# A two-layer decode kernel: the first feed-forward takes the up half by column blocks and w_out by matching row blocks, in turns

## The chip, the cores and the metric

The kernel runs on one core of a Trainium2 chip. Its engines are PE (TensorE, with its weight loads shown as PEld), DVE (VectorE), ACT (ScalarE), POOL (GpSimd) and SP (SyncE, which here issues nearly all DMAs). The metric is the device time of one execution in microseconds (us).

## The reference, cut to what matters

One token for each of two sequences passes twice through attention over a cache of 4096 keys and values (16 heads of 256) and a gated feed-forward of 448 to 1792 to 448. The same weights and caches serve both layers.

```python
def _A_ref(x, k_cache, v_cache, wq, wo):
    q = (x @ wq).reshape(B, Sq, H, Dh).transpose(0, 2, 1, 3)
    scores = jnp.einsum("bhqd,bhkd->bhqk", q, k_cache) * (Dh ** -0.5)
    o = jnp.einsum("bhqk,bhkd->bhqd", _softmax(scores), v_cache)
    return o.transpose(0, 2, 1, 3).reshape(B, Sq, H * Dh) @ wo
def _B_ref(x, W_gate, W_up, W_down):
    gate, up = x @ W_gate, x @ W_up
    return ((gate * (gate > 0)) * up) @ W_down
...
x = x + _A_ref(_layernorm(x), A_k_cache, A_v_cache, A_wq, A_wo)
x = x + _B_ref(_layernorm(x), B_W_gate, B_W_up, B_W_down)
# and the same two lines once more; B = 2, Sq = 1, D = 448, H = 16, Sk = 4096, Dh = 256, F = 1792, fp32
```

## The kernel before, in words

Everything that comes from memory lies in one large tile, `arena`, cut into 27 units (`Arena`, L49). A load takes a unit, or several, and the unit is free again when the last reader of the load is in the program. All loads stand in one list, `pending` (L267 and L268), in the order in which they are used. `release` (L206) frees a unit and calls `pump` (L138), which issues the next loads of the list on SP's queue as long as a unit is free. SP's DMA then waits on the chip for the readers of the unit that it overwrites. So each load is issued when an earlier piece has been read, and the loads start in the order of the list.

The program is: attention of layer 1 (32 pairs of head and sequence), the first feed-forward `ffn(False, oT)`, attention of layer 2, and the last feed-forward `ffn(True)`. Layer 2 starts with the pairs with which layer 1 ended, and the arena keeps part of their keys and values (`KEPT`, `LEFT`). Therefore few units circulate in the first feed-forward: the first four pieces of its weights go to four units, and each later piece waits for a release.

A piece of the feed-forward is 128 rows of 1792 floats (896 KB). There are seven pieces of `w_in` and four of `w_out`, the last of them half as large (`ffn_loads`, L247). Pieces 0 to 2 of `w_in` are the gate weights of three blocks of 128 input rows, piece 3 holds the last 64 input rows of gate and up together, and pieces 4 to 6 are the up weights. The hidden vector of 1792 is held as four groups of 448 columns on four groups of 32 partitions, so that four matmuls of 32 columns fill the array side by side (`proj`, L919). Between the gate pieces `arrive` (L939) adds the last head's output to the input.

The first feed-forward then works as follows. The gate sum `pg` goes through a ReLU on ACT into `hid` (L1023). The up sum `pu` is made of pieces 3, 4, 5 and 6 (L1024), with the sums of columns of the next query's weights (`add_up`, L978), the scale of the layer norm (`factors`, L1000) and a part of the output sum `y` put between them by `between` (L960). When all of `pu` is there, DVE multiplies 448 columns at once (L1025). PE turns `hid` by three transposes and two matmuls (L1035, L1037), DVE and ACT copy it back (L1041, L1046).

`w_out` lies by column blocks of the output (128, 128, 128 and 64 wide), each with all 1792 hidden rows as 14 chunks. `block` (L1051) adds 14 matmuls for a column block in the bank `po[1]`. After each block ACT copies it out with its sum (L1125), PE turns it into columns of `x` (L1137), DVE adds it (L1140), and `ask` (L1107) adds one step of the first query of layer 2, `q`. After the last block come the mean's part of the query (L1141), two last steps (L1114), a copy of the query (L496), and then the first scores of layer 2 on DVE (L592, and POOL at L499). Those scores read kept keys, and their readers are what the next loads wait for.

`acc` is the bank in which the heads' outputs are summed, on partitions 0 to 95 in three groups of 32; `y`, the running sum of the residual, is on two partitions from 96 on.

Of the kernel before, what the change touches and what calls it, by code (L numbers as in the profile page):

```python
# [81 lines left out]
def two_layers(  # L82
# [7 lines left out]
    w_out: bass.AP,  # L90
    out: bass.AP,
# [25 lines left out]
    def source(key, n):  # L117
        kind, name, c = key
        if kind in "kv":
            h, b = name  # L120
            at = (h * B + b + (kind == "v")) % (H * B)
            if name in spared and n == PAIR:
                return vk[at, :, VALUES * DH : PAIR * UNIT - KEYS * DH]
            size = F if key in left_at else n * UNIT
            c += NC * (kind == "k" and n < PAIR)
            return vk[at, :, c * UNIT : c * UNIT + size]
        if kind == "g":
            return w_pair[name - 1]
# [138 lines left out]
    pending += of_first + [(key, 1) for key in ffn_loads]  # L267
# [636 lines left out]
    def ffn(last, oT=None):  # L904
# [14 lines left out]
        def proj(p, parts):  # L919

            p = p[:, :D]
            for n, (part, c, done) in enumerate(parts):
# [11 lines left out]
                if not last and n == part and n + 2 <= FULL:  # L934
                    arrive(n + 2)
# [24 lines left out]
        def between(part, n):  # L960


            if last:
                if part in (4, 5):
                    busy(4 if part == 4 else 6)
            elif part == FULL and n == 0:
                factors()
                for i in range(2):
                    nc.tensor.matmul(
                        y, oT[:, i, :], wo[:, i * D : (i + 1) * D], start=False, stop=False  # L970
                    )
            elif part == 4:
                add_up(0)
                add_up(1)
            elif part == 5:
                add_up(2)
# [30 lines left out]

        if not last:
            arrive(0)
            arrive(1)  # L1010
        pg = proj(banks[0], [(0, 0, True), (1, 1, True), (2, 2, True), (3, 3, False)])
# [7 lines left out]
        else:  # L1019
            total = squares()  # L1020
            cols = room_q
        hid = row[:, :D]
        nc.scalar.activation(hid, pg, AF.Relu)  # L1023
        pu = proj(banks[1], [(3, 4, True), (4, 0, True), (5, 1, True), (6, 2, True)])  # L1024
        nc.vector.tensor_mul(hid, pu, hid)  # L1025
        if last:
            unit = ident[SUMS : SUMS + B, SUMS : SUMS + B]
            nc.tensor.matmul(y_left, unit, left, start=True, stop=False)
        else:
            add_up(FULL)  # L1030

        ph = banks[0][:, : FULL * P].rearrange("p (m r) -> p m r", m=FULL)
        ph_tail = small(P)
        for m in range(FULL):
            nc.tensor.transpose(ph[:, m, :], hid[:, m * P : (m + 1) * P], ident)  # L1035
        for half in (0, TAIL):
            nc.tensor.matmul(  # L1037
                ph_tail[half : half + TAIL], hid[:, FULL * P :], ident, start=True, stop=True
            )
        hT = row[:, : FULL * P].rearrange("p (m r) -> p m r", m=FULL)  # L1040
        nc.vector.tensor_copy(hT, ph)  # L1041

        tails = row[:, FULL * P : FULL * P + 64].rearrange("p (m r) -> p m r", m=2)
        for k, half in enumerate((slice(0, TAIL), slice(TAIL, P))):
            pairs = ph_tail[half].rearrange("p (m k r) -> p k m r", m=2, k=2)
            nc.scalar.activation(tails[half], pairs[:, k], AF.Copy)  # L1046
# [17 lines left out]
        if last:  # L1064


            square = little("square", B, bufs=1)
            nc.vector.tensor_mul(square, rstd, rstd)
            close = little("close", CLOSE, B, bufs=1)
            for i, st in enumerate(stat[-CLOSE:]):  # L1070
                nc.vector.tensor_mul(
                    close[:, i, :], square, st.rearrange("p (b r) -> p b r", b=B)[:, :, 0]
                )
            y_end = spare[1][SUMS : SUMS + B, :TAIL]
            nc.tensor.matmul(y_end, unit, y_end_row, start=True, stop=False)
            pds = [po[0][:, :D], spare[0][:, :D]] * 2

            def to_y(at, stop):
                nc.tensor.matmul(y[:, at], scaled, down[:, at], start=False, stop=stop)

            for c in range(FULL):
                at = block(pds[c], c, range(14))
                release("out", "", c)
                nc.scalar.activation(down[:, at], pds[c][:, at], AF.Copy)
                if c > 0:
                    to_y(before, False)
                before = at
            at = block(pds[FULL], FULL, range(14 - CLOSE))
            nc.scalar.activation(down[:, at], pds[FULL][:, at], AF.Copy)
            to_y(before, True)  # L1090
            nc.vector.tensor_copy(left, y_left)
            nc.sync.dma_start(found[:, : FULL * P], left)
            w = get("out", "", FULL)
            for i in range(CLOSE):
                k = 14 - CLOSE + i
                w_k = w[:, k * TAIL : (k + 1) * TAIL]
                nc.tensor.matmul(y_end, close[:, i, :], w_k, start=False, stop=False)
            nc.tensor.matmul(y_end, scaled, down[:, at], start=False, stop=True)
            nc.vector.tensor_copy(y_end_row, y_end)
            nc.scalar.dma_start(found[:, FULL * P :], y_end_row)  # L1100
            return

        q = po[0][:, :DH]

        def ask(c):  # L1107
            x_c = xT[:, c, b : b + 1].to_broadcast([P, P])
            if c < FULL:
                w_c = w_q[:, c * DH : (c + 1) * DH]  # L1110
                nc.tensor.matmul(q, x_c, w_c, start=(c == 0), stop=False)
            else:
                at = (c - FULL) * P
                nc.tensor.matmul(  # L1114
                    q[:, at : at + P], x_c, w_q[:, FULL * DH : FULL * DH + P],
                    start=False, stop=(c == FULL + 1),
                )

        pd = po[1][:, :D]
        sums = little("sums4", FULL + 1, bufs=1)  # L1120
        total = little("sums", 1)
        for c in range(FULL + 1):
            at = block(pd, c, range(14))
            release("out", "", c)
            nc.scalar.activation(down[:, at], pd[:, at], AF.Copy, accum_out=sums[:, c : c + 1])  # L1125
            if c > 0:
                ask(c - 1)
            else:
                add_up(FULL + 1)
            if c == FULL:  # L1130
                turn_cols = row[:, :DH]
                nc.vector.tensor_scalar_mul(turn_cols, cols, nscaled[:, b : b + 1])
                nc.vector.reduce_sum(total, sums, axis=AX.X)
            pt = small(B)
            found_in = [(spans[0][0], c)] if c < FULL else [(p, i.start) for p, i in spans[1:]]
            for p, _ in found_in:
                nc.tensor.matmul(pt[p], down[:, at], scaled, start=True, stop=True)  # L1137
            for p, i in found_in:
                x_c = xr[p, i]
                nc.vector.tensor_add(x_c, x_c, pt[p, :, None].to_broadcast(x_c.shape))  # L1140
        nc.tensor.matmul(q, total.to_broadcast([P, P]), turn_cols, start=False, stop=False)  # L1141
        for c in range(FULL, DC):
            ask(c)

        def center():
            minus = small(B)
            nc.tensor.matmul(minus, total.to_broadcast([P, P]), nscaled, start=True, stop=True)
            add_rows(P, scaled, down)
            less = little("less", B)
            nc.scalar.activation(less, minus, AF.Copy)  # L1150
            squared = little("total", B)
            unread = little("sq4", FULL + 1, bufs=1)
            for i in range(B):
                for p, c in spans:
                    x_c = xr[p, c, i]
                    nc.scalar.activation(x_c, x_c, AF.Identity, bias=less[p, i : i + 1])
                nc.scalar.activation(
                    unread, xT[:, : FULL + 1, i], AF.Square, accum_out=squared[:, i : i + 1]
                )
            nc.scalar.activation(xs[:, :, 32], xs[:, :, 31], AF.Copy)  # L1160
            return squared

        def rest_of_y():
            for c in range(2):
                nc.tensor.matmul(
                    y, oT[:, c, :], means[:, c : c + 1].to_broadcast([P, D]),
                    start=False, stop=False,
                )

        return q, center, rest_of_y  # L1170
# [76 lines left out]
```

## Time and profile before

| what | value |
|---|---|
| time, median of 3 runs | 1314.57 us (1314.09 to 1314.92) |
| the profiled execution's own time | 1314.77 us |
| span of its trace, first to last instruction | 1312.9 us |
| moved from memory | 559.55 MB, 426 GB/s over the span |
| busy share of the span | DVE 82%, PE 39%, POOL 22%, ACT 15% |
| DMA queue of SP | its packets fill 99.4% of 16 engines' span |
| feed-forward of layer 1 in the trace | gate from 665 us, first scores of layer 2 at 689.57 us |

The span is 1.9 us shorter than the time of the same execution. A busy share is an average over the whole span; what matters for the change is read from the 25 us between 665 and 690 us and from what follows. GB/s in a stretch counts the packets that start in it.

### The profile page before, as it was taken

The numbers are of one execution on the slowest core, as the hardware profiler recorded it, in microseconds if no ns is written. First come the engines' busy times: TensorE is split into PE (matmuls) and PEld (weight loads), VectorE is DVE, ScalarE is ACT, GpSimd is POOL, SyncE is SP. The second block draws the span as 40 slices with busy tenths as digits, with TensorE's granted clock in tenths as the row PEclk, the third lists the DMA queues.
The fourth block names the chain that finished last, engine by engine and source line by source line (L and its number), as shares of the span: only waits on it lengthen the run. The fifth ranks groups of instructions, "written<-read, shape, count | busy, mean of one in ns | idle before, by whom it ended". The sixth has DMA issues, their size and how long they took to land.

```text
span 1312.9 us, 8389 instructions
## 1 busy us (share of the span) xinstructions
PE 509.6 (39%) x3056; PEld 156.0 (12%) x3056; DVE 1078.9 (82%) x623; ACT 197.9 (15%) x803; POOL 289.3 (22%) x169
## 2 busy tenths in 40 slices
PE   3142243332433224324485544332343322433348
PEld 2010010010101001101141111000111000110013
DVE  4989989799897998788829798798999889886891
ACT  2100000010000000122417532000000000012231
POOL 0330412302023050021002235140345004100230
PEclk9676777657776567767697766666676667766569
DMA  9999999999999999999999999999999999999998
GB/s 407 437 434 428 438 432 429 437 426 430 444 423 436 441 434 416 446 420 428 421 375 412 433 430 438 437 432 428 429 438 430 437 430 429 440 429 425 434 421 331
DMA packets 20356, 560.09 MB, mean 427 GB/s; under 512 B 2264, under 2 KB 2396, under 8 KB 7260
## 3 DMA queue, kind: packets, MB, share of 16 engines
q1 hardware_dynamic: 20308, 559.56, 99.4%
q8 instruction: 24, 0.39, 0.1%
q14 instruction: 16, 0.13, 0.0%
q10 hardware_dynamic: 8, 0.00, 0.0%
HBM read 559.55 MB, written 0.00 MB: 426 GB/s over the span
## 4 chain that ended last, share of the span: by engine, by line
DMA 52%; DVE 33%; POOL 7%; PE 5%; issue 2%; ACT 1%; SPq 0%; POOLq 0%; DVEq 0%; ACTq 0%
DMA arena<-in_vk_dram 48%; DVE tiny L541 16%; DVE arena L527 10%; POOL tiny L643 5%; DVE arena L576 3%; DMA arena<-in_w_in_dram 3%; POOL tiny L615 2%; PE po L676 1%; DVE arena L592 1%; DMA arena<-in_w_out_dram 1%; PE small L709 1%; DVE tiny L589 1%; ACT arena L582 1%; DVE row L698 1%; DVE tiny L603 0%
## 5 line engine op out<-in xcount | busy, mean ns | idle before, releaser
L527 DVE TENSOR_TENSOR arena<-arena 128x8192 f32<-128x8192 f32 (+2 forms) x53 | 450.4, 8500 | 100.9 <-DMA arena<-in_vk_dram 99.6
L541 DVE TENSOR_REDUCE tiny<-arena 128x32 f32<-128x8192 f32 (+1 forms) x54 | 436.6, 8085 | 0.0
L676 PE MATMUL po<-arena,down 128*4 128x512 f32 x2044 | 316.6, 739 | 180.0 <-ACT down L631 110.6
L615 POOL PARTITION_ALL_REDUCE tiny<-tiny x63 | 96.0, 1524 | 711.9 <-DVE tiny L609 711.2
L709 PE MATMUL small<-tiny,row 128*128 128x2 f32 x124 | 30.6, 351 | 566.7 <-DVE row L698 566.7
L643 POOL PARTITION_ALL_REDUCE tiny<-tiny x63 | 165.3, 2623 | 60.3 <-ACT down L631 60.3
L627 ACT ACTIVATE tiny<-tiny 128x1 f32<-128x1 f32 x63 | 18.5, 294 | 723.7 <-POOL tiny L615 723.7
L676 PEld LDWEIGHTS po<-arena,down 128*4 128x4 f32 x2044 | 66.9, 98 | 401.0 <-issue 229.4
L709 PEld LDWEIGHTS small<-tiny,row 128*128 128x128 f32 x124 | 27.9, 314 | 595.9 <-DVE row L698 595.9
L582 ACT ACTIVATE arena<-arena 128x256 f32<-128x256 f32 x142 | 57.1, 404 | 44.5 <-DVE arena L576 43.6
L456 PE MATMUL po<-arena,xs 128*33 128x512 f32 (+1 forms) x130 | 62.8, 640 | 0.0
L468 POOL PARTITION_BROADCAST arena<-arena x32 | 21.8, 749 | 176.3 <-ACT arena L464 165.5
L732 PE MATMUL acc<-arena,tiny 128*2 128x448 f32 x124 | 50.0, 903 | 23.3 <-DVE tiny L722 23.3
L533 ACT ACTIVATE arena<-arena 128x256 f32<-128x256 f32 x112 | 44.8, 402 | 79.9 <-DVE arena L527 79.9
L576 DVE TENSOR_TENSOR arena<-arena 128x2048 f32<-128x2048 f32 (+2 forms) x21 | 40.2, 1913 | 2.9 <-PE acc L732 2.9
L464 ACT ACTIVATE arena<-po 33x512 f32<-33x512 f32 x13 | 7.7, 590 | 174.6 <-PE po L456 174.6
L722 DVE TENSOR_TENSOR tiny<-small,tiny 128x4 f32<-128x4 f32 x31 | 5.0, 162 | 28.0 <-PE small L709 28.0
L631 ACT ACTIVATE down<-tiny 128x32 f32<-128x32 f32 x64 | 26.6, 415 | 2.2
L582 ACT ACTIVATION_READ_ACCUMULATOR arena<-arena 128x1 f32 x142 | 26.5, 187 | 0.0
L698 DVE SCALAR_TENSOR_TENSOR row<-po,tiny,row 128x256 f32<-128x256 f32 x32 | 15.3, 479 | 13.2 <-ACT row L694 13.1
L456 PEld LDWEIGHTS po<-arena,xs 128*33 128x33 f32 x130 | 16.0, 133 | 59.9 <-issue 57.1
L609 DVE TENSOR_REDUCE tiny<-tiny 128x1 f32<-128x32 f32 x64 | 11.9, 186 | 11.8 <-ACT arena L582 8.5
(207 smaller groups left out, 356.4 us busy)
## 6 DMA issues: line engine op xcount, KB each, us to landing
arena<-in_vk_dram SPq DMA_DIRECT2D x17, 4096.0 KB, 38.8
arena<-in_vk_dram SPq DMA_DIRECT2D x16, 2048.0 KB, 31.1
arena<-in_w_pair_dram SPq DMA_DIRECT2D x11, 1792.0 KB, 30.8
arena<-in_w_in_dram SPq DMA_DIRECT2D x12, 896.0 KB, 25.6
arena<-in_vk_dram SPq DMA_DIRECT2D x10, 1024.0 KB, 9.3
arena<-in_vk_dram SPq DMA_DIRECT2D x1, 6528.0 KB
arena<-in_w_head_dram SPq DMA_DIRECT2D x7, 896.0 KB, 31.5
arena<-in_w_out_dram SPq DMA_DIRECT2D x5, 896.0 KB, 8.5
```

Source lines behind the costliest of these rows:

```text
L456: nc.tensor.matmul(q[:, cols], xs[:, c, :], w_c, start=(i == 0), stop=(i == len(parts) - 1))
L527: nc.vector.tensor_mul(part, part, q_of[u][:, None, :].to_broadcast([P, n, DH]))
L533: nc.scalar.activation(kt[:, t, :], kt[:, t, :], AF.Copy, accum_out=s_of[u][:, t : t + 1])
L541: nc.vector.reduce_sum(found, part, axis=AX.X)
L576: nc.vector.tensor_mul(part[:, :whole, :], kt[:, :whole, :], q_of[u][:, None, :].to_broadcast([P, whole, DH]),)
L582: nc.scalar.activation(part[:, t, :], part[:, t, :], AF.Copy, accum_out=found[:, t : t + 1])
L615: nc.gpsimd.partition_all_reduce(mx_of[u], mx, P, RED.max)
L643: nc.gpsimd.partition_all_reduce(total[:, b : b + 1], rs, P, RED.add)
L676: nc.tensor.matmul(po_of[u][32 * t : 32 * t + 4, (i - 2 * t) * DH : (j - 2 * t) * DH], p_of[u][:, at : at + 4], values[:, i * DH : j * DH] ...
L698: nc.vector.scalar_tensor_tensor(row[:, :DH], po_of.pop(u)[:, DH:], fold[:, 1:2], row[:, :DH], op0=ALU.mult, op1=ALU.add,)
L709: nc.tensor.matmul(pT_of[u][:, c, :], row[:, c * P : (c + 1) * P], pick[:, b : b + B], start=True, stop=True,)
L732: nc.tensor.matmul(acc[at : at + B], oT_of[h][:, c, :], wo[:, c * D : (c + 1) * D], start=(n < 3), stop=(n >= n_u - (5 if settle else 3)),)
```

## The change

The loads of the first feed-forward get another order and two new arrays: `w_up` (the up half by blocks of 128 hidden columns of each of the four groups, and one piece with the 64 last rows of gate beside the last 64 columns of up) and `w_down` (`w_out` by rows: four chunks of 128 hidden rows with all 448 output columns in a piece, the last piece two chunks). The pieces have the sizes of before and their number is 11 as before; the last feed-forward still reads `w_in` and `w_out`.

In the middle, for each block m of hidden columns: the up sum of these columns (`up`), a multiplication by DVE of 128 columns, one transpose, a copy by ACT, and four matmuls 448 wide with piece m of `w_down`. These add in partitions 0 to 95 of `acc`, whose sum stays open from the first turn to the last. After the last turn all four column blocks of that sum are copied, turned and added to `x` one after the other, and the query is asked.

```diff
+        if kind == "up":
+            return w_up[:, c * F : (c + 1) * F]
+        if kind == "dn":
+            return w_down[:, 4 * D * c : min(4 * D * (c + 1), 14 * D)]
...
-    pending += of_first + [(key, 1) for key in ffn_loads]
+    at_turn = [*ffn_loads[:FULL], ("up", "", FULL)]
+    at_turn += [(kind, "", m) for m in range(FULL) for kind in ("up", "dn")] + [("dn", "", FULL)]
+    pending += of_first + [(key, 1) for key in at_turn]
...
+        def tail_of(out, w, width):
+            for j in range(4):
+                i = j % 2 * width
+                nc.tensor.matmul(
+                    out[32 * j : 32 * j + 32, :], xs[:, FULL + j // 2, :32], w[:, i : i + width],
+                    start=False, stop=True,
+                )
+
+        def middle(hid, ph, hT, tails, turn_tail):
+            q = po[0][:, :DH]
+            pu = po[1][:, :D]
+            pd = acc[:SUMS]
+            def up(m, w):
...
+                for c in range(FULL):
+                    for j in range(4):
+                        i = (4 * c + j) * width
+                        nc.tensor.matmul(
+                            pu[32 * j : 32 * j + 32, at], xs[:, c, :32], w[:, i : i + width],
+                            start=(c == 0), stop=False,
+                        )
+                tail_of(pu[:, at], w[:, 4 * FULL * width :], width)
+                nc.vector.tensor_mul(hid[:, at], pu[:, at], hid[:, at])
+                return at
+            up(FULL, get("up", "", FULL)[:, F // 2 :])
+            release("up", "", FULL)
+            factors()
...
+            for m in range(FULL + 1):
+                if m < FULL:
+                    at = up(m, get("up", "", m))
+                    release("up", "", m)
+                    add_up((0, 1, 4)[m])
+                    if m == 0:
+                        turn_tail()
+                    nc.tensor.transpose(ph[:, m, :], hid[:, at], ident)
+                    nc.scalar.activation(hT[:, m, :], ph[:, m, :], AF.Copy)
+                    stat = [hT[:, m, 32 * j : 32 * j + 32] for j in range(4)]
+                else:
+                    nc.vector.tensor_scalar_mul(turn_cols, cols, nscaled[:, b : b + 1])
+                    stat = [tails[:, i, :] for i in range(2)]
...
+                w = get("dn", "", m)
+                for j, st in enumerate(stat):
+                    k = 4 * m + j
+                    g = 32 * (k % 3)
+                    nc.tensor.matmul(
+                        pd[g : g + 32], st, w[:, j * D : (j + 1) * D], start=(k < 3), stop=(k > 10)
+                    )
+                release("dn", "", m)
...
+            for c in range(FULL + 1):
+                at = slice(c * P, c * P + (P if c < FULL else TAIL))
+                nc.scalar.activation(
+                    down[:SUMS, at], pd[:, at], AF.Copy, accum_out=sums[:SUMS, c : c + 1]
+                )
...
+                for p, _ in found_in:
+                    nc.tensor.matmul(
+                        pt[p], down[:SUMS, at], scaled[:SUMS], start=True, stop=True
+                    )
...
+                if c > 0:
+                    ask(c - 1)
...
-        for c in range(FULL + 1):
-            at = block(pd, c, range(14))
             release("out", "", c)
-            nc.scalar.activation(down[:, at], pd[:, at], AF.Copy, accum_out=sums[:, c : c + 1])
...
```

In SP's queue this is the stretch from the first weights of the feed-forward to the first loads of layer 2. Before it reads:

```order
L162 DMA arena<-in_w_in_dram 128x1792 x7
L162 DMA arena<-in_w_out_dram 128x1792 x3
L162 DMA arena<-in_w_out_dram 128x896
L162 DMA arena<-in_w_head_dram 128x1792
L162 DMA arena<-in_vk_dram 128x1792 x2
L162 DMA arena<-in_w_head_dram 128x1792
```

And now:

```order
L168 DMA arena<-in_w_in_dram 128x1792 x3
L168 DMA arena<-in_w_up_dram 128x1792 x2
L168 DMA arena<-in_w_down_dram 128x1792
L168 DMA arena<-in_w_up_dram 128x1792
L168 DMA arena<-in_w_down_dram 128x1792
L168 DMA arena<-in_w_up_dram 128x1792
L168 DMA arena<-in_w_down_dram 128x1792
L168 DMA arena<-in_w_down_dram 128x896
```

The pieces have the same sizes; from the fifth on, one of the up half and one of `w_out` alternate, and the four loads of layer 2 after them stand as before.

On PE this is the stretch from the up half to the end of the hidden work (`po_102` holds the up sum and then, before, the output's blocks; `acc` the heads' sums; `pq` the sums of the query's columns). Before:

```order
L925 MATMUL po_102<-arena,xs 32x448 x4
L982 MATMUL pq<-arena,tiny 128x256
L925 MATMUL po_102<-arena,xs 32x448 x4
L988 MATMUL pq<-arena,tiny 128x128
L1035 MATMUL po_101<-ident,row 128x128 x3
L1037 MATMUL small<-ident,row 64x128 x2
L1058 MATMUL po_102<-arena,row 32x128 x14
```

Now, from the second turn on:

```order
L1027 MATMUL po_102<-arena,xs 32x128 x12
L1009 MATMUL po_102<-arena,xs 32x128 x4
L978 MATMUL pq<-arena,tiny 128x256
L1052 MATMUL po_101<-ident,row 128x128
L978 MATMUL pq<-arena,tiny 128x256
L1066 MATMUL acc<-arena,row 32x448 x4
L984 MATMUL pq<-arena,tiny 128x128
L1027 MATMUL po_102<-arena,xs 32x128 x12
```

The transposes and the output matmuls moved between the up blocks, so that PE comes to the next up block only behind the output matmuls of the turn.

On PE again, the end of the feed-forward (`small` holds the turned columns of `x`, `po_101` the query). Before:

```order
L1058 MATMUL po_102<-arena,row 32x128 x14
L1111 MATMUL po_101<-arena,xs 128x256
L1137 MATMUL small<-tiny,down 128x2
L1058 MATMUL po_102<-arena,row 32x64 x14
L1111 MATMUL po_101<-arena,xs 128x256
L1137 MATMUL small<-tiny,down 64x2 x2
L1141 MATMUL po_101<-row,tiny 128x256
```

And now:

```order
L1066 MATMUL acc<-arena,row 32x448 x6
L1099 MATMUL small<-tiny,down 128x2 x2
L1079 MATMUL po_101<-arena,xs 128x256
L1099 MATMUL small<-tiny,down 128x2
L1079 MATMUL po_101<-arena,xs 128x256
L1099 MATMUL small<-tiny,down 64x2 x2
L1079 MATMUL po_101<-arena,xs 128x256
L1107 MATMUL po_101<-row,tiny 128x256
```

The turning of all four column blocks and the steps of the query moved behind the last output matmul; before, three of the four stood between the blocks.

## Rows read from the trace of the kernel before

**Rows 1.** The page: span, SP's DMA queue, and the chain by engine.
```profile
span 1312.9 us, 8389 instructions
...
q1 hardware_dynamic: 20308, 559.56, 99.4%
...
DMA 52%; DVE 33%; POOL 7%; PE 5%; issue 2%; ACT 1%; SPq 0%; POOLq 0%; DVEq 0%; ACTq 0%
```

**Rows 2.** Busy time by stretch (PE, PEld, DVE, ACT, POOL), granted clock, DMA share, GB/s.
```profile
400.00:500.00 100.00, 34.68 (x168) 9.30 (x169) 87.05 (x24) 5.67 (x19) 29.36 (x12) 0.64 1.01 436
...
666.00:672.00 6.00, 5.05 (x54) 2.17 (x54) 0.97 (x6) 1.18 (x2) 0.00 (x0) 1.00 0.90 331
672.00:682.00 10.00, 8.08 (x72) 3.39 (x67) 1.84 (x6) 1.34 (x4) 0.00 (x0) 1.00 1.01 414
682.00:690.00 8.00, 7.95 (x113) 5.50 (x113) 2.39 (x11) 2.13 (x12) 0.37 (x1) 1.00 0.94 315
690.00:694.00 4.00, 4.00 (x23) 2.90 (x22) 4.00 (x23) 3.67 (x19) 4.00 (x3) 1.00 1.00 412
...
710.00:760.00 50.00, 24.56 (x122) 6.03 (x122) 41.94 (x71) 29.27 (x136) 10.97 (x10) 0.75 1.02 432
```

**Rows 3.** SP's DMA issues in order of time: start, duration, what.
```profile
674.18 0.33 SPq L162 DMA_DIRECT2D arena<-in_w_out_dram  x1
...
676.16 0.33 SPq L162 DMA_DIRECT2D arena<-in_w_out_dram  x1
...
678.91 0.33 SPq L162 DMA_DIRECT2D arena<-in_w_out_dram  x1
...
682.02 0.33 SPq L162 DMA_DIRECT2D arena<-in_w_head_dram  x1
683.87 2.18 SPq L162 DMA_DIRECT2D arena<-in_vk_dram  x2
687.20 0.33 SPq L162 DMA_DIRECT2D arena<-in_w_head_dram  x1
690.36 29.86 SPq L162 DMA_DIRECT2D arena<-in_vk_dram  x17
```

**Rows 4.** Line 162 in the window of the issue at 674.18 us.
```profile
DMA to landing us min/median/max: 8.1/8.1/8.1
```

**Rows 5.** PE's instructions in order of time; in brackets the idle time before.
```profile
669.78 1.71 PE L925 MATMUL po<-arena,xs 128*32 128x448 f32 x16 [0.95 <-DMA arena<-in_w_in_dram]
...
677.92 0.96 PE L925 MATMUL po<-arena,xs 128*32 128x448 f32 x8 [1.19 <-DMA arena<-in_w_in_dram]
...
680.19 0.44 PE L1037 MATMUL small<-ident,row 128*64 128x128 f32 x4
680.91 1.07 PE L1058 MATMUL po<-arena,row 128*32 128x128 f32 x28 [0.28 <-DVE row L1041]
```

**Rows 6.** DVE's instructions in order of time.
```profile
673.54 0.17 DVE L1006 TENSOR_SCALAR tiny<-tiny 128x2 f32<-128x2 f32 x1
678.97 0.62 DVE L1025 TENSOR_TENSOR row<-po,row 128x448 f32<-128x448 f32 x1 [5.26 <-PE po L925]
```

**Rows 7.** ACT's instructions in order of time.
```profile
682.03 0.28 ACT L1125 ACTIVATE down<-po 128x128 f32<-128x128 f32 x1 [0.90 <-PE po L1058]
682.20 0.19 ACT L1125 ACTIVATION_READ_ACCUMULATOR down<-po 128x1 f32 x1
...
687.21 0.22 ACT L1125 ACTIVATE down<-po 128x64 f32<-128x64 f32 x1 [1.05 <-PE po L1058]
```

**Rows 8.** The chain of waits from 676 to 700 us: start, us, what.
```profile
686.59 0.57 PE po L1058 x28
...
689.57 7.96 DVE arena L592 x46
```

**Rows 9.** The chain of waits over the whole span, after the feed-forward.
```profile
768.61 8.65 POOL tiny L615
...
803.96 25.68 DMA arena<-in_vk_dram
```

More of the change, by code (lines that the diff above doesn't have):

```diff
@@ L90, in two_layers @@
     w_out: bass.AP,
+    w_up: bass.AP,
+    w_down: bass.AP,
     out: bass.AP,
@@ L933, in proj @@
                     release("in", "", part)
-                if not last and n == part and n + 2 <= FULL:
+                if not last and n + 2 <= FULL:
                     arrive(n + 2)
@@ L960, in between @@
         def between(part, n):
[L963 to L976, printed above, removed]
+            if last and part in (4, 5):
+                busy(4 if part == 4 else 6)
         def add_up(c):
@@ L1010, in ffn @@
             arrive(1)
-        pg = proj(banks[0], [(0, 0, True), (1, 1, True), (2, 2, True), (3, 3, False)])
+        parts = [(0, 0, True), (1, 1, True), (2, 2, True), (3, 3, False)]
+        pg = proj(banks[0], parts if last else parts[:FULL])
         if last:
@@ L1019, in ffn @@
         else:
+            tail_of(pg, get("up", "", FULL)[:, : F // 2], D)
             total = squares()
@@ L1023, in ffn, with turn_tail @@
         nc.scalar.activation(hid, pg, AF.Relu)
+        ph = banks[0][:, : FULL * P].rearrange("p (m r) -> p m r", m=FULL)
+        hT = row[:, : FULL * P].rearrange("p (m r) -> p m r", m=FULL)
+        tails = row[:, FULL * P : FULL * P + 64].rearrange("p (m r) -> p m r", m=2)
+        def turn_tail():
+            ph_tail = small(P)
+            for half in (0, TAIL):
+                nc.tensor.matmul(
+                    ph_tail[half : half + TAIL], hid[:, FULL * P :], ident, start=True, stop=True
+                )
+            for k, half in enumerate((slice(0, TAIL), slice(TAIL, P))):
+                pairs = ph_tail[half].rearrange("p (m k r) -> p k m r", m=2, k=2)
+                nc.scalar.activation(tails[half], pairs[:, k], AF.Copy)
+        if not last:
+            return middle(hid, ph, hT, tails, turn_tail)
         pu = proj(banks[1], [(3, 4, True), (4, 0, True), (5, 1, True), (6, 2, True)])
         nc.vector.tensor_mul(hid, pu, hid)
[L1026 to L1033, printed above, removed]
+        unit = ident[SUMS : SUMS + B, SUMS : SUMS + B]
+        nc.tensor.matmul(y_left, unit, left, start=True, stop=False)
         for m in range(FULL):
             nc.tensor.transpose(ph[:, m, :], hid[:, m * P : (m + 1) * P], ident)
[L1036 to L1040, printed above, removed]
         nc.vector.tensor_copy(hT, ph)
[L1043 to L1046, printed above, removed]
+        turn_tail()
         stat = [hT[:, m, 32 * j : 32 * j + 32] for j in range(4) for m in range(FULL)]
@@ L1062, in block @@
             return at
[L1064 to L1101, printed above, removed]
@@ L1105, in ffn @@
[L1105 to L1117, printed above, removed]
@@ L1119, in ffn @@
-        pd = po[1][:, :D]
-        sums = little("sums4", FULL + 1, bufs=1)
-        total = little("sums", 1)
-        for c in range(FULL + 1):
-            at = block(pd, c, range(14))
+        square = little("square", B, bufs=1)
+        nc.vector.tensor_mul(square, rstd, rstd)
+        close = little("close", CLOSE, B, bufs=1)
+        for i, st in enumerate(stat[-CLOSE:]):
+            nc.vector.tensor_mul(
+                close[:, i, :], square, st.rearrange("p (b r) -> p b r", b=B)[:, :, 0]
+            )
@@ L1124, in ffn, with to_y @@
+        y_end = spare[1][SUMS : SUMS + B, :TAIL]
+        nc.tensor.matmul(y_end, unit, y_end_row, start=True, stop=False)
+        pds = [po[0][:, :D], spare[0][:, :D]] * 2
+        def to_y(at, stop):
+            nc.tensor.matmul(y[:, at], scaled, down[:, at], start=False, stop=stop)
+        for c in range(FULL):
+            at = block(pds[c], c, range(14))
             release("out", "", c)
-            nc.scalar.activation(down[:, at], pd[:, at], AF.Copy, accum_out=sums[:, c : c + 1])
+            nc.scalar.activation(down[:, at], pds[c][:, at], AF.Copy)
@@ L1126, in ffn @@
             if c > 0:
[L1127 to L1170, printed above, removed]
+                to_y(before, False)
+            before = at
+        at = block(pds[FULL], FULL, range(14 - CLOSE))
+        nc.scalar.activation(down[:, at], pds[FULL][:, at], AF.Copy)
+        to_y(before, True)
+        nc.vector.tensor_copy(left, y_left)
@@ L1172, in two_layers @@
+        nc.sync.dma_start(found[:, : FULL * P], left)
+        w = get("out", "", FULL)
+        for i in range(CLOSE):
+            k = 14 - CLOSE + i
+            w_k = w[:, k * TAIL : (k + 1) * TAIL]
+            nc.tensor.matmul(y_end, close[:, i, :], w_k, start=False, stop=False)
+        nc.tensor.matmul(y_end, scaled, down[:, at], start=False, stop=True)
+        nc.vector.tensor_copy(y_end_row, y_end)
+        nc.scalar.dma_start(found[:, FULL * P :], y_end_row)
     found = out.rearrange("b s d -> (b s) d")
@@ L1211, in _arrays, with packed @@
     chunks += [np.concatenate([down[j, rows:], down[j + 1, rows:]]) for j in (0, 2)]
+    def packed(w, at, width):
+        w = w.reshape(D, 4, D)[:, :, at : at + width]
+        tail = w[rows:].reshape(TAIL, 2, 2 * width).transpose(1, 0, 2).reshape(P, 2 * width)
+        return [w[c * P : (c + 1) * P].reshape(P, 4 * width) for c in range(FULL)] + [tail]
+    ups = [part for m in range(FULL) for part in packed(B_W_up, m * P, P)]
+    ups += packed(B_W_gate, 0, D)[FULL:] + packed(B_W_up, rows, TAIL)
+    in_rows = [chunks[j * FULL + m] for m in range(FULL) for j in range(4)] + chunks[4 * FULL :]
     found = {
@@ L1220, in _arrays @@
         ),
+        "w_up": np.concatenate(ups, axis=1),
+        "w_down": np.concatenate(in_rows, axis=1),
     }
```

66 lines of the change are left out of this document (added).

## The prediction

> **What bounds the kernel now.** I read the page first. SP's DMA queue fills 99.4% of the span, while no engine stands near that; the chain of waits lies 52% on DMA and 33% on DVE [rows 1]. So memory sets the time, and a change of the feed-forward is worth what it does to the flow of bytes. The second view is the busy time by stretches. In the middle of layer 1 the core moves 436 GB/s. With the feed-forward's pieces the undisturbed rate is 414 GB/s (672 to 682 us), and in two stretches it falls: 331 GB/s from 666 to 672 us, and 315 GB/s from 682 to 690 us [rows 2]. Against 414 the first loses (414 - 331) / 414 x 6 = 1.2 us, the second (414 - 315) / 414 x 8 = 1.9 us. These 3.1 us are all that a better order of this feed-forward can give back to the flow of its own weights.
>
> The third view, SP's issues, shows where the second hole comes from. The issue at 678.91 is followed by one at 682.02, then 683.87, 685.72 (the second of the pair) and 687.20 [rows 3]: each waits for a unit whose reader is a block of the output, and those start only when the whole hidden vector is turned. The first hole comes before the up half, from the release of gate pieces, which the change leaves alone. So only the hole of 1.9 us is in play, plus what a later start of layer 2 costs behind it: the next issue, at 690.36, is released by the first scores of layer 2.
>
> **What stays.** The same 11 pieces of the same sizes pass through the same four units, so no bytes are added. The gate, its 1.2 us hole, both attentions and the last feed-forward are as before. PE stands at the full granted clock, 1.00, in all four stretches from 666 to 694 us [rows 2]; it is as busy in the new order, so I leave its clock out.
>
> **Prices of one turn.** An up block is 16 matmuls of 128 columns, 32 records; 28 records of the same width took 1.07 us, so 1.22 us [rows 5]. The multiplication of 128 columns lies between 0.17 (2 columns) and 0.62 us (448 columns) [rows 6]; by the line between them 0.30. A transpose: two matmuls of that kind took 0.44 [rows 5], one at least 0.22; I take 0.38, since one alone has nothing to overlap with. ACT's copy of 128 by 128 takes 0.28 [rows 7]. The four output matmuls share three groups of partitions, so one group is used twice. Eight records of 448 columns, once round four groups, took 0.96, sixteen, twice round, 1.71 [rows 5]; I take 1.71. Four hand-overs stand in front of the output matmuls; in rows 5 to 6 the DVE instruction began 0.09 us after the matmuls in front of it ended (677.92 + 0.96 to 678.97), so 0.1 each. From the landing of an up piece to the release of the output piece behind it: 1.22 + 0.30 + 0.38 + 0.28 + 0.4 + 1.71 = 4.29 us. Two pieces of 917,504 bytes take 4.43 us at 414 GB/s. The turn keeps pace with its loads, with 0.14 us to spare.
>
> The Trainium skill's page on TensorEngine Tiling (Array Packing), section Overview, gives a factor of up to 4 for stationary operands of at most 32 columns. By that rule the new output matmuls, on three groups in place of four, would lose a third: 14/3 in place of 14/4 rounds, 0.9 us more at 0.75 us a round. The rows say otherwise for this kernel: 56 matmuls of the old form cost up to four times 1.07 us, about 38 ns a record whatever the width, and 14 wide ones on three groups cost 14/3 x 0.75 = 3.5 us.
>
> **The release times.** Turn 0: `factors` keeps DVE until 673.71 [rows 6]; then 0.30 + 0.38 + 0.28 + 0.3 + 1.71 give 676.7 for the release that issued at 676.16 before: 0.5 later, but then several pieces stand in the queue. Turn 1: piece 6 landed at 677.9 [rows 5], its place in the queue is now the second up block's. Its release comes at 677.9 + 1.2 = 679.1 (678.91 before) and that of its output piece at 677.9 + 4.29 = 682.2 (682.02 before). Turn 2: the third up block has the place of the piece issued at 674.18, which landed 8.1 us later, at 682.3 [rows 3, 4]. PE is just free of turn 1. Releases: 682.3 + 1.22 = 683.5 (before 683.87), then 682.3 + 4.29 = 686.6 (before 685.72), and the last half piece, whose two matmuls fit into the open groups of the second round, about 686.8 (before 687.20).
>
> So the four issues in the hole move by +0.2, -0.4, +0.9 and -0.4 us. The gap of 3.1 us between 678.91 and 682.02, from which the hole begins, stays at 3.1 us (679.1 to 682.2). The reason is that a turn is fed by landings 2.2 us apart, and those are set by the queue, not by PE.
>
> **The start of layer 2.** Before, the last block's matmuls ended at 687.16, ACT's copy began at 687.21, and the first scores at 689.57 [rows 7, 8]: 2.36 us from the last copy to the scores. Now all four copies come behind the last output matmul. Copy and read of the sum take 0.36 us together (682.03 to 682.39) [rows 7]; the first begins at 686.85, the fourth three steps later, at 687.93. With the same 2.36 us the scores begin at 690.29, 0.7 us later. Before, the copies of three blocks lay beside the matmuls of the next; that cover is gone. Behind the scores wait the 17 loads that began to issue at 690.36 [rows 3].
>
> **What this costs the flow.** The shift of +0.2 at the head of the hole costs 0.2, the -0.4 behind it gives 0.4 back: together -0.2. The last -0.4 stands behind the late one and gives nothing. The +0.9 has no row of its own: it costs nothing if enough stands in the queue, as between 687.20 and 690.36, where 3.2 us without an issue left 412 GB/s [rows 2, 3], and 0.9 if nothing does, as after 678.91. I take 0.4, nearer to the first, since two pieces stand before it. The 0.7 us later start lies between 0 and 0.7; again three pieces stand before it, but that cover was used up to the last 3.2 us; I take 0.4. Sum: -0.2 + 0.4 + 0.4 = +0.6 us. The ends: -0.4, where only the gain counts, and +1.6, which is -0.2 + 0.9 + 0.7 and 0.2 for the column sums that stand on PE inside turn 1. DVE itself is no bound here: from 803.96 us the chain waits 25.7 us for a load [rows 9], so scores that begin 0.7 us later only matter through the units they free.
>
> The profiled execution took 1314.77 us, 0.2 above the median of the runs; 1.9 us of it lie outside the span and stay. 1314.77 + 0.6 = 1315.4, and at the median 1314.57 + 0.6 = 1315.2 us.
>
> **Rivals.** First, the turns fill the hole. If the up pieces land a us earlier than at 677.9 and 682.3, each output piece is read at once, the issue of 682.02 comes a us earlier, and all 1.9 us return: 1312.7. For it speaks that PE now frees an up unit 1.2 us after landing, where the piece that landed at 682.3 kept its unit until the issue at 683.87, 1.6 us [rows 3, 4]. Against it: four units and landings 2.2 us apart fix the turn.
>
> Second, slower: the turn falls behind its loads. It crosses PE, DVE, PE, ACT, PE one after the other where before one crossing served all. Its margin is 0.14 us. From the point at which the four hand-overs and the transpose cost more than 0.14 us above my prices, each later landing adds its delay to the next. At 0.3 us a hand-over a turn takes 5.1 us, 0.7 over the pace; three turns make 2.0, the start of layer 2 adds its 0.7: 1314.57 + 2.7 = 1317.3. The hand-over of 0.09 speaks against it; that PE reaches the next up block only behind the output matmuls speaks for it.
>
> Third, nothing reaches the end: 690 to 694 us ran at 412 GB/s [rows 2], and from 710 to 760 us the flow is at 432, so units may be plentiful and a shift of 0.7 vanish: 1314.6. This is also the case in which the alternation does not do what it is written for, because the order of landings sets all releases.
>
> **How the numbers follow.** The forecast (1314.2 to 1316.2) has 0.45, the third rival 0.22, the first 0.18, the slower one 0.15. About 0.2%, 2.6 us, is what a measurement can tell from no change. Faster by more than that asks for 1311.9, which even the filled hole doesn't reach; with the first hole added it would, so 0.04. Slower by more begins at 1317.2, half of the second rival: 0.08. Same: 0.88. The range takes in most of both rivals: 1312.7 to 1317.0.
>
> **What the profile will show.** Right, if 682 to 690 us moves about 315 GB/s again, the issue of the first load of layer 2 stands near 682.2, an output turn takes about 1.7 us on PE, and the first scores start near 690.3. Wrong in the flow, if that stretch moves over 380 GB/s (first rival) or if the issues drift later from turn to turn (second). Wrong in the step on the start of layer 2, if the scores begin before 689.6 or after 691.5. Wrong altogether, if a stretch outside 665 to 720 us changes.

## The result and the profile after

The changed kernel took 1316.96 us, the median of 20 runs (1315.63 to 1319.45), beside 1314.03 us for the kernel before, also 20 runs on the same chip. The ratio is 1.0022 with a 95% interval of 1.0015 to 1.0029: slower by 2.9 us [2.0, 3.8], where the forecast was 0.6. The profiled execution took 1315.79 us, near the fastest of its kernel, while that of before, 1314.77 us, stands 0.7 us above the median of its kernel beside it. So the two traces show a smaller loss, 1.0 us.

The page after, the same lines as [rows 1]: the span, SP's DMA queue, and the chain by engine.

```profile
span 1313.9 us, 8422 instructions
...
q1 hardware_dynamic: 20308, 559.56, 99.5%
...
DMA 53%; DVE 31%; POOL 7%; PE 6%; issue 2%; ACT 1%; SPq 0%; POOLq 0%; DVEq 0%; ACTq 0%
```

The same bytes pass through the same queue, and DMA still bounds the kernel. The stretches, with the columns of [rows 2]:

```profile
666.00:672.00 6.00, 5.26 (x79) 2.45 (x79) 1.19 (x8) 0.58 (x2) 0.00 (x0) 1.00 0.89 325
672.00:682.00 10.00, 8.87 (x99) 4.14 (x99) 1.34 (x7) 2.49 (x6) 0.00 (x0) 1.00 1.00 401
682.00:690.00 8.00, 6.70 (x66) 3.85 (x65) 1.77 (x8) 1.35 (x9) 0.00 (x0) 1.00 0.99 380
690.00:694.00 4.00, 4.00 (x22) 2.86 (x21) 2.93 (x16) 2.71 (x14) 2.39 (x2) 1.00 0.92 371
...
710.00:760.00 50.00, 22.06 (x130) 5.67 (x122) 42.86 (x74) 29.28 (x136) 12.04 (x11) 0.76 1.02 433
```

The hole of before at 682 to 690 us reads 380 in place of 315 GB/s, and a new one stands behind it: 690 to 694 fell from 412 to 371. From 710 to 760 us the flow is as before. Two wider stretches set the one against the other. Before (not among the rows above):

```profile
660.00:690.00 30.00, 26.39 (x284) 14.19 (x276) 6.84 (x29) 5.13 (x18) 0.37 (x1) 1.00 0.97 371
690.00:720.00 30.00, 18.79 (x97) 6.28 (x96) 29.06 (x125) 22.38 (x102) 7.95 (x9) 0.77 1.02 411
```

And after:

```profile
660.00:690.00 30.00, 26.14 (x294) 13.71 (x287) 6.05 (x29) 4.90 (x17) 0.00 (x0) 1.00 0.98 384
690.00:720.00 30.00, 18.31 (x107) 7.06 (x105) 28.38 (x121) 21.76 (x99) 8.11 (x8) 0.87 0.99 378
```

The feed-forward's own 30 us moved (384 - 371) / 371 x 30 = 1.1 us more bytes, the 30 us behind them (411 - 378) / 411 x 30 = 2.4 us fewer. The loss lies at the start of layer 2. SP's issues after, which answer to [rows 3]:

```profile
677.22 1.62 SPq L168 DMA_DIRECT2D arena<-in_w_down_dram  x2
681.80 0.33 SPq L168 DMA_DIRECT2D arena<-in_w_head_dram  x1
683.34 3.16 SPq L168 DMA_DIRECT2D arena<-in_vk_dram  x2
686.60 0.38 SPq L168 DMA_DIRECT2D arena<-in_w_head_dram  x1
692.29 7.61 SPq L168 DMA_DIRECT2D arena<-in_vk_dram  x7
```

The first line is the last two output pieces of the feed-forward. The four loads of layer 2 behind them stand within some 0.4 us of the predicted times; only the last line, released by the first scores, is late: 692.29 where it was 690.36. The chain of waits from the last output matmuls to the scores, which answers to [rows 8], says why (start, us, what):

```profile
684.48 1.99 PE acc L1066 x12
686.47 0.02 issue
686.49 1.08 ACT down L1091 x8
687.57 0.09 issue
687.66 0.35 PE small L1099 x2
688.01 0.54 PE po L1079 x2
688.55 0.19 PE small L1099 x2
688.74 0.54 PE po L1079 x2
689.28 0.21 PE small L1099 x4
689.50 0.63 PE po L1079 x2
690.12 0.43 PE po L1107 x2
690.56 0.46 PE po L1082 x4
...
691.50 7.96 DVE arena L600 x46
```

The copies (L1091) are done by 687.57, before the prediction lets the fourth begin (687.93). From there the chain lies on PE until 691.02, with only the copy of the query on DVE behind it: turning a column block into `x` (L1099) and asking its columns (L1079), block after block, then the mean's step (L1107) and the asks of the upper columns (L1082). Before, three of the four turnings and two of the three wide asks lay between the blocks of the output, and 2.41 us passed from the last output matmul (687.16) to the scores (689.57). The scores begin at 691.50, 1.93 us later than before.

### The profile page after: what moved, and what is told of

The parts are those of the page before. It is cut to its first block, busy times and chain, and to the rows that moved or that the text cites. A ratio compares the mean times of both kernels' runs of the same rounds, so it can differ in the third digit from the quotient of the medians.

```text
span 1313.9 us, 8422 instructions
## 1 busy us (share of the span) xinstructions
PE 513.1 (39%) x3068; PEld 157.3 (12%) x3068; DVE 1078.7 (82%) x625; ACT 198.5 (15%) x806; POOL 307.5 (23%) x169
## 4 chain that ended last, share of the span: by engine, by line
DMA 53%; DVE 31%; POOL 7%; PE 6%; issue 2%; ACT 1%; SPq 0%; POOLq 0%; DVEq 0%; ACTq 0%
DMA arena<-in_vk_dram 49%; DVE tiny L549 15%; DVE arena L535 10%; POOL tiny L651 4%; POOL tiny L623 3%; DVE arena L584 2%; DMA arena<-in_w_in_dram 2%; PE po L684 2%; DMA arena<-in_w_out_dram 1%; DVE arena L600 1%; PE small L717 1%; DVE tiny L597 1%; DMA arena<-in_w_up_dram 1%; ACT arena L590 1%; DVE row L706 0%
## 5 line engine op out<-in xcount | busy, mean ns | idle before, releaser
L623 POOL PARTITION_ALL_REDUCE tiny<-tiny x63 | 113.1, 1795 | 710.0 <-DVE tiny L617 709.3
L651 POOL PARTITION_ALL_REDUCE tiny<-tiny x63 | 166.4, 2641 | 60.4 <-ACT down L639 60.4
L590 ACT ACTIVATION_READ_ACCUMULATOR arena<-arena 128x1 f32 x142 | 26.6, 187 | 0.0
L541 ACT ACTIVATION_READ_ACCUMULATOR arena<-arena 128x1 f32 x112 | 21.0, 187 | 0.0
```

Of the source, the lines that this page charges most:

```text
L541: nc.scalar.activation(kt[:, t, :], kt[:, t, :], AF.Copy, accum_out=s_of[u][:, t : t + 1])
L590: nc.scalar.activation(part[:, t, :], part[:, t, :], AF.Copy, accum_out=found[:, t : t + 1])
L623: nc.gpsimd.partition_all_reduce(mx_of[u], mx, P, RED.max)
L651: nc.gpsimd.partition_all_reduce(total[:, b : b + 1], rs, P, RED.add)
```

## Experiments

The theory of the late start: what the changed kernel loses is the later start of layer 2, and each us of it costs up to a us, since the loads behind it wait for units that the scores free. Against it stand two others: the turns themselves cost, or a later start costs next to nothing and the difference lies in the runs.

### e1_same: the changed kernel again

No edit.

> The changed kernel once more, for a second trace and its time on this chip. Its scores of layer 2 began at 691.50 us, 1.93 us later than before. Theory A (the later start of layer 2 makes the loss, since the next 17 loads wait for the units that its scores free): 2 to 3.5 us above before, and a hole of 250 to 350 GB/s behind 690 us again. Theory B (the turns make it: output pieces are released late, the start is hidden): the same time, and the missing bytes lie between 666 and 690 us.

1316.5 us (12 runs), ratio 1.0017 [1.0005, 1.0029] to 1314.13 of before. DVE's first score instruction, and the stretch behind it:

```profile
691.98 0.42 DVE L600 SCALAR_TENSOR_TENSOR arena<-arena,po 128x256 f32<-128x256 f32 x1
```

```profile
690.00:720.00 30.00, 18.50 (x108) 7.47 (x108) 28.27 (x121) 21.38 (x97) 8.10 (x8) 0.89 0.96 364
```

The late start and the poor flow behind it come back: 2.4 us later than before and 364 GB/s, in an execution of 1316.45 us. So the loss is no accident of one comparison.

### e2_delay3 and e3_delay9: the kernel before, with only the start delayed

```diff
+        for _ in range(3):
+            busy(4)
         nc.tensor.matmul(q, total.to_broadcast([P, P]), turn_cols, start=False, stop=False)
```

In e3_delay9 it is `range(9)`. `busy` puts idle matmuls on PE, here ahead of the mean's step at the end of the feed-forward.

> The kernel before, with three idle matmuls (2 by 256, into an unread bank) put on PE ahead of the last steps of the first query of layer 2. They should delay its scores by about 1.9 us, as in the changed kernel, and move nothing before. Theory A: 1.5 to 2.5 us slower than before, with a hole in the flow behind 690 us. Theory B: within 0.5 us of before.

> The same with nine idle matmuls, a delay of about 5 to 6 us. It gives the price of a us of later start. Theory A: 4.5 to 6 us slower than before, nearly a us for each. Theory B: at most 2 us slower, since the queue holds three pieces at that point.

Three of them moved the scores by 1.28 us, less than the 1.9 meant; nine by 4.81, of which 0.84 had been there ahead of the delay: in that execution the first load of layer 2 already issued at 682.86, behind a stretch from 666 to 672 us at a granted clock of 0.50, the lower level of 1.2 GHz. PE had been busy 7.46 of the 8 us from 655 to 663 us at 1.00; the record of before has no such fall. In e3_delay9:

```profile
666.00:672.00 6.00, 6.00 (x40) 2.17 (x36) 0.97 (x6) 0.00 (x0) 0.00 (x0) 0.50 0.78 268
690.00:720.00 30.00, 22.32 (x112) 8.35 (x113) 25.50 (x109) 19.77 (x90) 8.11 (x8) 0.77 0.94 353
```

The medians: 1315.74 us, ratio 1.0006 [0.9996, 1.0017], and 1318.1 us, ratio 1.0026 [1.0015, 1.0037]. In us the ratios are 0.8 [-0.5, 2.2] and 3.4 [2.0, 4.9] above before. So e3_delay9 falls between its two theories, below the 4.5 that A asked for and above the 2 of B: by the ratios a us of later start costs 0.6 to 0.7 us, not nearly a us. SP's issues in e2_delay3:

```profile
681.92 0.33 SPq L162 DMA_DIRECT2D arena<-in_w_head_dram  x1
683.77 2.18 SPq L162 DMA_DIRECT2D arena<-in_vk_dram  x2
687.10 0.33 SPq L162 DMA_DIRECT2D arena<-in_w_head_dram  x1
```

Its stretches:

```profile
666.00:672.00 6.00, 5.83 (x59) 2.24 (x59) 1.13 (x7) 1.32 (x2) 0.00 (x0) 1.00 0.85 299
682.00:690.00 8.00, 7.95 (x113) 5.32 (x113) 1.54 (x7) 1.35 (x8) 0.00 (x0) 1.00 1.01 386
660.00:690.00 30.00, 27.22 (x291) 14.32 (x281) 6.13 (x27) 4.42 (x14) 0.00 (x0) 1.00 0.97 378
690.00:720.00 30.00, 19.57 (x104) 6.61 (x102) 29.03 (x125) 22.42 (x102) 8.11 (x8) 0.83 0.99 385
```

Two things are to be seen. The start alone, without any turn, takes the flow of 690 to 720 us from 411 to 385 GB/s (353 in e3_delay9): that speaks against a start that costs nothing. The ratio of e3_delay9 shows a price, though e2_delay3's by itself is still in reach of no change. And the hole of 682 to 690 us is gone (386 GB/s) in a kernel whose feed-forward is that of before and whose issues stand within 0.1 us of [rows 3]. It had lost bytes earlier instead, 299 in place of 331 GB/s from 666 to 672; over the 30 us it moved 378, before 371. So the 380 of the changed kernel doesn't show that the turns filled a hole.

### e4_no_ask: the turns without the three wide asks

```diff
-                pt = small(B)
+                pt = small(B) if c % 2 == 0 else po[1][:, :B]
...
-                if c > 0:
-                    ask(c - 1)
             nc.tensor.matmul(
-                q, total.to_broadcast([SUMS, P]), turn_cols[:SUMS], start=False, stop=False
+                q, total.to_broadcast([SUMS, P]), turn_cols[:SUMS], start=True, stop=False
```

> The changed kernel without the three wide steps of the query of layer 2 (the query of the first pair lacks the first 384 rows of its input), and with the turned column blocks in two banks by turns, so that none waits for the addition of the one ahead. Loads, turns and releases of the feed-forward stay. The scores should begin near 690.0 us in place of 691.5. Theory A: 1 to 2 us faster than the changed kernel, that is 0.5 to 2 us above before. Theory B: as slow as the changed kernel, 2.5 to 3.5 us above before.

This is the run that parts the late start from the turns. 1314.67 us, ratio 1.0004 [0.9995, 1.0013], beside 1316.5 us of e1_same, which differs from it only in the end of the feed-forward; the profiled execution took 1314.47. Its scores and its flow:

```profile
689.56 0.42 DVE L600 SCALAR_TENSOR_TENSOR arena<-arena,po 128x256 f32<-128x256 f32 x1
```

```profile
682.00:690.00 8.00, 6.85 (x68) 3.86 (x60) 2.61 (x12) 2.07 (x13) 0.32 (x1) 1.00 0.95 339
660.00:690.00 30.00, 26.75 (x282) 13.31 (x274) 6.59 (x31) 5.63 (x21) 0.32 (x1) 0.94 0.98 380
690.00:720.00 30.00, 16.44 (x97) 5.97 (x96) 29.06 (x125) 22.38 (x102) 8.01 (x9) 0.84 1.01 401
```

All turns are there, the scores begin where they did before (689.56, before 689.57), and the time is that of before. The interval reaches from a gain of 0.7 us to a cost of 1.7 us: that the turns make the whole loss falls, and so does a gain of 1.9 us by a filled hole. A smaller share of either is not excluded.

### e5_a_less and e6_b_less: an earlier start, with and without turns

In the changed kernel, behind the last output matmul:

```diff
...
+            for c in range(FULL, DC):
+                ask(c)
...
-                pt = small(B)
...
-                if c > 0:
-                    ask(c - 1)
-            nc.tensor.matmul(
-                q, total.to_broadcast([SUMS, P]), turn_cols[:SUMS], start=False, stop=False
-            )
...
```

In the kernel before:

```diff
...
-            if c > 0:
-                ask(c - 1)
-            else:
+            if c == 0:
                 add_up(FULL + 1)
             if c == FULL:
+                for i in range(FULL, DC):
+                    ask(i)
...
-        nc.tensor.matmul(q, total.to_broadcast([P, P]), turn_cols, start=False, stop=False)
...
```

> The changed kernel with the turning of its output sum into x, the three wide steps of the query of layer 2 and its mean's step left out (x of layer 2 lacks the feed-forward, the query most of its input). Loads, turns and releases stay; the scores should begin near 688.2 us, 1.4 us earlier than in the kernel before. Theory A (the start of the scores sets the issues of the next 17 loads, and the turns' fuller flow counts only if the start is early as well): 0.5 to 1.5 us faster than before. Theory B (the turns themselves cost time): at or above before.

> The kernel before with the three wide steps and the mean's step of the query left out, so that its scores begin 1 to 2 us earlier (near 688 us) while its turned hidden vector and column blocks stay. Theory A: at most 0.8 us faster, since the hole of 1.9 us ahead of 690 us stays and only 0.7 us were lost behind it. A symmetric price (each us of start is worth 0.7 us in both directions): 1 us or more faster.

Both start the scores at the same time, 688.41 and 688.42, some 1.2 us earlier than before. The profiled executions took 1312.35 and 1312.55 us. The medians: 1313.25, ratio 0.9987 [0.9976, 0.9999], and 1314.0, ratio 0.9996 [0.9983, 1.0010]. The stretch behind the start in e5_a_less:

```profile
690.00:720.00 30.00, 15.36 (x95) 5.34 (x93) 29.06 (x122) 21.79 (x101) 8.01 (x9) 0.86 1.02 411
```

And in e6_b_less:

```profile
690.00:720.00 30.00, 16.47 (x97) 6.23 (x96) 29.06 (x122) 21.73 (x100) 7.76 (x9) 0.90 1.02 422
```

With the start equal, turns and no turns again agree within 0.2 us in the traces. By the medians they stand 0.75 us apart, by the ratios 1.2, and the intervals overlap; whether the turns help a little once the start is early stays open. The interval of e6_b_less takes in both of its theories, so it doesn't settle the price of an earlier start.

### e7_up_blocks: half of the change

The up half in column blocks; the output by columns and the end of `middle` are those of before. The list of loads:

```diff
-    at_turn += [(kind, "", m) for m in range(FULL) for kind in ("up", "dn")] + [("dn", "", FULL)]
+    at_turn += [("up", "", m) for m in range(FULL)] + ffn_loads[7:]
```

> One part of the change alone: the up half by column blocks, each multiplied and turned at once, but all of w_out behind it by column blocks of the output as before, in its own bank, with the copies and steps of the query between the blocks. The hidden vector is turned about 0.7 us earlier than before (near 680.2 us), so the first output piece is released near 681.3 and the scores start near 689. Theory A: 0 to 1.2 us faster than before, at least 2 us faster than the changed kernel. Theory B, if the up blocks are what costs: as slow as the changed kernel.

1314.57 us, ratio 0.9996 [0.9983, 1.0008]. The scores began at 689.97, not at 689: PE waits for the second and third output pieces, as its rows show:

```profile
682.88 1.07 PE L1080 MATMUL po<-arena,row 128*32 128x128 f32 x28 [0.64 <-DMA arena<-in_w_out_dram]
685.07 1.07 PE L1080 MATMUL po<-arena,row 128*32 128x128 f32 x28 [0.27 <-DMA arena<-in_w_out_dram]
```

So in this execution the start is tied to the landing of the output pieces, and an earlier turning of the hidden vector gains nothing. With the short end of before and the new up blocks the time is that of before.

### e8_banks: is the long end PE's, or a wait between PE and DVE?

The turned blocks by turns in two banks, as in the first edit of e4_no_ask alone.

> The changed kernel with its four turned column blocks in two banks by turns (one look). In its trace each turning matmul behind the last output matmul waits for DVE's addition of the block ahead, 0.73 us a block, with a step of the query in between. If that alternation makes the long end, the scores begin 0.7 us or more earlier against the last output matmul; if the query's five steps and the mean's step on PE make it (some 3.2 us in a row), they begin at most 0.4 us earlier, 4.7 to 5.1 us after the last output matmul.

One run: 1315.3 us, before 1315.17. The last output matmuls and the scores:

```profile
684.59 1.96 PE L1066 MATMUL acc<-arena,row 128*32 128x448 f32 x12 [1.05 <-DMA arena<-in_w_down_dram]
```

```profile
691.25 0.42 DVE L600 SCALAR_TENSOR_TENSOR arena<-arena,po 128x256 f32<-128x256 f32 x1
```

From 686.55 to 691.25 are 4.7 us, where the changed kernel took 691.50 - 686.44 = 5.06. The shared bank costs some 0.4 us, by one execution each. Of the 4.7 us the chain has PE from 687.02 to 690.77 with one gap of 0.03 us; ACT's first copy ahead of it and DVE's copy of the query behind it take nearly all the rest. So the long end is in the main PE's own work.

### All of them in one table

Sorted by the start of the scores (us); the time is that of the same profiled execution.

| kernel | scores begin | GB/s, 690 to 720 | time | ratio to before |
|---|---|---|---|---|
| e5_a_less | 688.41 | 411 | 1312.35 | 0.9987 |
| e6_b_less | 688.42 | 422 | 1312.55 | 0.9996 |
| e4_no_ask | 689.56 | 401 | 1314.47 | 1.0004 |
| before | 689.57 | 411 | 1314.77 | 1 |
| e7_up_blocks | 689.97 | 392 | 1314.14 | 0.9996 |
| e2_delay3 | 690.85 | 385 | 1315.85 | 1.0006 |
| e8_banks | 691.25 | 374 | 1315.30 | one run only |
| changed | 691.50 | 378 | 1315.79 | 1.0022 |
| e1_same | 691.98 | 364 | 1316.45 | 1.0017 |
| e3_delay9 | 694.38 | 353 | 1319.46 | 1.0026 |

A straight line through start and time has a slope of 1.10 us per us (1.04 without e3_delay9), with a scatter of 0.4 us around it, whether a kernel has turns or not. So in the traces the start of layer 2 costs about its own length. By the many runs behind the ratios this is less sure: through the eight ratios the slope is 0.83, through the four kernels without turns (before, e6_b_less, e2_delay3, e3_delay9) 0.68, and through the four with all of them (changed, e1_same, e4_no_ask, e5_a_less) 1.17. Each start is known from one execution, so whether turns make a late start dearer stays open.

## Why the prediction was right in sign and short in size

**The time: inside its range by luck.** 1316.96 us lies 0.04 us below the top of the range, and it does so because the kernel before took 1314.03 us beside it, not the 1314.57 on which the prediction was built. The change cost 2.9 us, where the sum had 0.6 and its upper end 1.6. The time lies above the forecast's own stretch (1314.2 to 1316.2), and by the prediction's bar of 2.6 us it is slower, for which it gave 0.08. The nearest number, 1317.3, is that of the second rival, whose mechanism did not occur.

**The release times: right.** Predicted 682.2, 683.5, 686.6 and 686.8; measured 681.80, 683.34, 686.18 (the second of the pair) and 686.60. An output turn was to take 1.71 us, and the second took 1.66 on PE:

```profile
680.10 1.66 PE L1066 MATMUL acc<-arena,row 128*32 128x448 f32 x8
```

From the start of its up block at 677.82 to the issue at 681.80 that turn took 3.98 us, priced at 4.29. The copies began at 686.49, predicted 686.85. That the turn keeps pace with its loads held, so the slower rival, a turn that falls behind, is refuted.

**The step that failed: "with the same 2.36 us the scores begin at 690.29".** The fourth copy began at 687.25 (predicted 687.93), and the scores at 691.50: 4.25 us where 2.36 were carried over. ACT's row of that copy:

```profile
687.25 0.22 ACT L1091 ACTIVATE down<-acc 96x64 f32<-96x64 f32 x1
```

The prediction moved the copies behind the last matmul, but not what hangs on them: three turnings of column blocks and two of the three wide asks (an ask takes 0.54 us on the chain), which before lay between the blocks of the output. The rows of the order ahead of the prediction show exactly these instructions moving; they were not priced. The term was mis-sized: +1.93 us (2.4 in e1_same) in place of +0.7. The prediction's own limit for this step, scores after 691.5, was reached, and passed in e1_same (691.98).

**Its price: probably too low.** 0.4 us of 0.7, some 0.57 per us, against 0.83 by the ratios and 1.10 by the traces of the table. The delays of the kernel before alone (0.6 and 0.7 by their ratios) do not refute 0.57. The prediction counted three pieces in the queue as cover; with the next release 5.3 us behind the last issue (686.60 + 0.38 to 692.29) that cover is used up. 1.93 x 0.83 to 1.93 x 1.10 make 1.6 to 2.1 us, where 2.9 [2.0, 3.8] was measured over the runs (2.2 [0.7, 3.8] in e1_same) and 1.0 between the two traces. So the later start accounts for more than half of the median loss; where the rest, about a us, comes from stays open, since e4_no_ask leaves room for a cost of the turns.

**The hole at 682 to 690 us: a wrong reading that cost nothing.** "Moves about 315 GB/s again" was wrong, at 380, the very limit from which the prediction spoke of the first rival. But 315 was no property of the kernel: e2_delay3 has 386 there with the same issues. The first rival (1312.7) took it for 1.9 us to be won. e4_no_ask, with all turns and the start of before, still has 339 there; it moved 380 over the 30 us, 0.7 us more bytes than before, and its time is that of before. So the 1.9 us did not return; a gain of up to 0.7 us would not be seen.

**The third rival, nothing reaches the end (1314.6): refuted** by the ratio, and by the table, in which the end follows the start.

**The price of the output matmuls.** All 28 records of the new form took 1.69 + 1.66 + 1.96 = 5.31 us on PE in three goes (from 675.50, 680.10 and 684.48 us; a few records of other sums lie inside the first), where before the four blocks took at most 4 x 1.07 = 4.28 [rows 5]. The aside's estimate of 3.5 us in all was wrong twice: 38 ns a record does not hold whatever the width, since its own rows have 0.96 / 8 = 0.12 us at 448 columns [rows 5], and 14 matmuls in goes of 4, 4 and 6 are six rounds of three groups, not 14/3. A turn's four matmuls on three groups took 1.66 us, where four groups once round took 0.96 [rows 5]. The sum of the prediction used 1.71 a turn and doesn't suffer from this. The prediction set the loss of a third aside that it drew from the Trainium skill (TensorEngine Tiling (Array Packing), Overview), which gives a factor of up to 4 at 32 columns. The trace agrees with it in direction: at least 5.31 - 4.28 = 1.03 us more, where the prediction worked out 0.9 by it.

## What to carry to other kernels

When a stage is cut so that its last part comes later, list everything that hung on the part's earlier end, not only the first instruction behind it, and price the whole tail on the engine that runs it. Where loads are released by compute, a later start of the next stage is not hidden: here each us cost some 0.7 to 1.2 us. A rate in a stretch of some us, of one execution, is no property of a kernel; compare it over the whole stage, and with a second execution of the same instructions.

## What the runs showed that was not expected

- With issues within 0.1 us of each other, the same stretch moved 315 GB/s in one execution and 386 in another; a part of the difference had been lost earlier (331 and 299 GB/s from 666 to 672 us).
- Three calls of `busy(4)`, 1.46 us on PE, moved the scores by 1.28 us only.
- Matmuls 32 columns by 448 on three groups took 5.31 us for 28 records, 190 ns each; those of 448 columns on four groups took 107 ns each (16 in 1.71 us), those of 128 columns 38 ns each (28 in 1.07 us). A cost by the record holds for one width and one set of groups only.
